# Top-32 attention followed by a quick-GELU block on one core: the division moved behind the value products, q and k turned by DMA, a second bank for the first layer, and a new order of a pair of slots

## The chip, the core and the metric

The kernel runs on one NeuronCore of one Trainium2 chip. The engines are TensorE (PE, with its weight loads as PEld), VectorE (DVE), ScalarE (ACT), GpSimd (POOL) and SyncE (SP), which issues DMAs. Each engine takes its instructions in the order in which the program gives them, and an instruction that waits holds up all that stand behind it on that engine. The metric is the device time of one execution in microseconds (us), as the median of several runs.

## The reference

Eight batches of eight heads, 576 positions, 64 values per head. Each row of scores keeps its 32 largest entries, is softmaxed over them and multiplied with v; the heads are put side by side (512 wide), and two dense layers with a gate follow.

```python
batch, n_heads, seq, head_dim = (8, 8, 576, 64)
n_tokens, d_model, d_ff = (4608, 512, 2048)
...
scores = scale * np.matmul(q, k.transpose(0, 1, 3, 2))
kth = np.partition(scores, -top_k, axis=-1)[..., -top_k:-top_k + 1]      # top_k = 32
scores = np.where(scores >= kth, scores, -1000000000.0)
attn = np.exp(scores - np.max(scores, axis=-1, keepdims=True))
attn = attn / (np.sum(attn, axis=-1, keepdims=True) + 1e-09)
x = np.matmul(attn, v)                       # heads side by side: (4608, 512)
h = x @ w_in
g = h * (1.0 / (1.0 + np.exp(-1.702 * h)))
return g @ w_out
```

## The kernel before

**Slots.** Attention is cut into 144 slots, 18 for each batch. A slot has 128 query rows of a pair of heads (`hp`, four pairs), so it has two score rows of 576 on each partition. Sixteen slots of a batch take the first 512 rows (`t` = 0 to 3 by `hp`), and two take the last 64 rows of two head pairs each ("ends" slots). Four slots with the same `t` make one tile `xT` of 128 tokens by 512 for the dense layers; the ends of two batches together make one tile `xT_t`. That gives 36 token tiles. The first layer of a tile is made in four groups (`hidden`, `ph`, 16 products in the program), and each group is projected by the second layer (`project`, `po`, four products in the program). So there are 144 groups of each, as many as slots. All products are in float32, and the trace counts each of them twice, except transposes: a group of `ph` is x32 there and a group of `po` x8.

**What a slot does.** `scores` (L240, PE) fills four banks of PSUM; `copy_scores` (L251, ACT) brings them to `sc`; `topk` (L260, L263, DVE) finds the 32 largest by four rounds of MAX8 and three of MATCH_REPLACE8 on each of the two rows; `bounds` (L279, L280, POOL) makes two numbers per row of them; `exponentials` (L288, L291, ACT) turns all scores below the 32nd to zero weight, takes the exponentials into `pr` and sums them into `den`; `divide` (L300, L302 on DVE, L310 on POOL) multiplies the whole of `pr` with the inverse of `den`; `turn_by_dma` has ACT put the low and the high halves of the words apart (L344), writes them to DRAM (L346, SP) and reads them back turned (L348, SP) into `pt`; `values` (L363, PE) multiplies with v; `bring` (L378 or L383, ACT) copies the result into `xT`. The first layer is followed by `tanh` and a copy of `ph` to `h` (L430, L433, ACT), by `gate` (L442, L443, POOL; L445 on DVE at the start and end) and by `project`; after four projections ACT copies `po` to `ob` (L465) and SP sends it out (L467).

**Order.** All orders are written out by hand. `slot(n)` handles slots 0 to 11, in which the weights are also rounded and `pr` is turned by PE (L322, L325). From slot 12 on, `two_slots(n)` handles slots n and n+1, 66 times, and two more times for what is left over; `last_slot` finishes the dense layers. In `two_slots`, the exponentials of slot n-1 come first, then `find(n)` runs on DVE with `divide(n-1)` after its seventh operation; in the second half the same follows for n and n+1. `values` takes slots n-4 and n-3. q and k of a later head pair are loaded at the slots in `FETCH` and turned by PE and ACT (`prepare`, L208 to L217) at the slots in `READY`.

**Buffers that matter.** `ps_h` has one bank, so a group of `ph` can't begin before ACT has read the last one. `ps_t` has two banks, for transposes and for `o` of `values`. `ps_p` has one for `po`. `pt` has two buffers, `sc` four, `pr` two.

Of the kernel before, what the change touches and what calls it, by code (L numbers as in the profile page):

```python
# [30 lines left out]
def kernel(  # L31
# [71 lines left out]
    apart = pool("apart", 4, space=DRAM)  # L103
    ps_s = pool("ps_s", 2, space=PSUM)
# [65 lines left out]
    def load(name, b, hp, queue=None):  # L170

        src = q if name == "q" else k
        t = loads.tile([P, NF, 2, D] if queue is None else [P, 2, NF, D], F32, name=f"{name}_l")
        heads_of = (lambda j: t[:, :, j, :]) if queue is None else (lambda j: t[:, j, :, :])
# [4 lines left out]
        if ("ends", b, hp) not in loaded:  # L179
            loaded["ends", b, hp] = loads.tile([P, 2, D], F32, name="ends")  # L180
        on = slice(0, TAIL) if name == "q" else slice(TAIL, P)
        queue.dma_start(
            loaded["ends", b, hp][on, :, :], src[b, 2 * hp : 2 * hp + 2, FULL:S, :].rearrange("h p d -> p h d")
        )
        loaded[name, b, hp] = t
# [14 lines left out]
    def prepare(name, b, hp):  # L200
        src = loaded.pop((name, b, hp))


        before = 0 if name == "q" else TAIL
        dst = qkt.tile([P, S + before], F32, name=f"{name}_t")
        full = ps_t.tile([P, 512], F32, name="tp")
        for t in range(NF):
            nc.tensor.transpose(full[:, t * P : (t + 1) * P], src[:, t, :, :], ident[:])  # L208
        scale = SCALE if name == "q" else 1.0
        nc.scalar.mul(out=dst[:, before : before + FULL], in_=full[:], mul=scale)  # L210
        (qT if name == "q" else kT)[b, hp] = dst
        if name == "k":
            ends = ps_t.tile([P, 512], F32, name="tp")
            nc.tensor.transpose(ends[:, 0:P], loaded.pop(("ends", b, hp))[:], ident[:])
            nc.scalar.mul(out=qT[b, hp][:, FULL:S], in_=ends[:, 0:TAIL], mul=SCALE)
            for to in (0, before + FULL):
                nc.scalar.copy(out=dst[:, to : to + TAIL], in_=ends[:, TAIL:P])  # L217


    slots = []  # L220
    for b in range(B):
# [3 lines left out]
        slots += ends + full if b % 2 else full + ends  # L225
# [21 lines left out]
    def copy_scores(n):  # L247
        ps = st[n].pop("ps")
        sc = st[n]["sc"] = scp.tile([P, 2, S], F32, name="sc")
        for i in range(2):  # L250
            nc.scalar.copy(out=sc[:, i, :].rearrange("p (c k) -> p c k", c=2), in_=ps[i][:, :, 0:HALF])  # L251
# [30 lines left out]
    def exponentials(n, between=lambda: None):  # L282
# [3 lines left out]
        den = st[n]["den"] = small.tile([P, 2], F32, name="den")  # L286
# [9 lines left out]
    def divide(n):  # L296

        den, pr = st[n]["den"], st[n]["pr"]
        some = small.tile([P, 2], F32, name="some")
        nc.vector.tensor_scalar_add(some[:], den[:], 1e-9)  # L300
        rden = small.tile([P, 2], F32, name="rden")
        nc.vector.reciprocal(rden[:], some[:])  # L302
        if n < SETTLED:
            by = st[n]["by"] = xtt.tile([P, 2, P], F32, name="by", tag="xT_t")
            for i in range(2):
                nc.gpsimd.tensor_scalar(by[:, i, :], ident[:], rden[:, i : i + 1], None, op0=ALU.mult)
        else:
            for i in range(2):
                on = slice(i * S, (i + 1) * S)
                nc.gpsimd.tensor_scalar(pr[:, on], pr[:, on], rden[:, i : i + 1], None, op0=ALU.mult)  # L310
# [29 lines left out]
    def turn_by_dma(n):  # L340
# [4 lines left out]
        rows = apart.tile([P, 2, 2 * S], U16, name="rows")  # L345
        nc.sync.dma_start(rows[:], halves)  # L346
        pt = st[n]["pt"] = ptp.tile([P, 2 * NF + 1, P], F32, name="pt")
# [4 lines left out]
    def values(n, put_off=None):  # L352
# [20 lines left out]
        def bring():  # L373
# [10 lines left out]
            if hps[-1] == NP - 1:  # L384
                if t < NF:
                    to = out[b * S : b * S + FULL, :].rearrange("(p t) c -> p t c", t=NF)[:, t, :]
                    ready.append((xts.pop((b, t)), [(slice(0, P), to)]))
                elif b % 2:
                    first = [(b - 1 + i) * S + FULL for i in range(2)]
                    rows = [(slice(i * TAIL, (i + 1) * TAIL), out[x : x + TAIL, :]) for i, x in enumerate(first)]  # L390
                    ready.append((xts.pop((b // 2, t)), rows))
# [6 lines left out]

    ready = []
# [4 lines left out]
    def hidden():  # L404
# [4 lines left out]
        ph = ps_h.tile([P, G, P], F32, name="ph")  # L409
# [15 lines left out]
    def tanh(aside):  # L425

        if to_gate:
            ph, g, rows = to_gate.pop()
# [21 lines left out]
    def project(blocks):  # L450
# [12 lines left out]
        if blocks[-1] == G - 1 and g == NG - 1:  # L463
            ob = thp.tile([P, C], F32, name="ob", tag="th")
            nc.scalar.mul(out=ob[:], in_=po[:], mul=0.5 / RAISE**2)  # L465
            for on, to in rows:
                nc.sync.dma_start(to, ob[on, :])  # L467
# [10 lines left out]
    READY = (((-9, -8), (-7, -6), (-4, -3), (-2, -1)), ((-8, -7), (-6, -5), (-4, -3), (-4, -3)))  # L478
    FETCH = (((-13, -12), (-11, -10), (-7, -7), (-5, -4)), ((-12, -11), (-10, -9), (-6, -6), (-5, -5)))
    VALUES = ((-8, -7, 2, 2), (-8, -7, 3, 3))  # L480
# [13 lines left out]
    for b in range(1, B):  # L494
        for hp in range(NP):
            for i, name in enumerate("qk"):
                at(b * PER + FETCH[b % 2][hp][i], load, name, b, hp)
                at(b * PER + READY[b % 2][hp][i], prepare, name, b, hp)
            at(b * PER + VALUES[b % 2][hp], load_v, b, hp)
# [16 lines left out]
    def prepare_first():  # L516

        qt = qT[0, 0] = qkt.tile([P, S], F32, name="q_t")
# [259 lines left out]
```

## Time and profile before

| | |
|---|---|
| median of 3 runs | 1820.0 us (1819.95 to 1821.7) |
| the profiled execution | 1822.16 us, of which the span of its instructions is 1820.4 us |
| PE busy | 1563.9 us (86% of the span) |
| DVE busy | 1449.2 us (80%) |
| ACT busy | 1151.6 us (63%) |
| POOL busy | 969.0 us (53%) |
| granted TensorE clock, mean | 0.93 |
| queue of SP | 42.5% of 16 DMA engines' span |

The profile page gives busy time by engine, the span in 40 slices, the DMA queues, a chain of work followed back from the last instruction, and groups of instructions by line with the idle time before them and its releaser. A timeline row has the start, the duration, the engine, the line, the operation, the count and in brackets the idle time of the engine before it with the releaser.

### The profile page before, as it was taken

The numbers are of one execution on the slowest core, as the hardware profiler recorded it, in microseconds if no ns is written. First come the engines' busy times: TensorE is split into PE (matmuls) and PEld (weight loads), VectorE is DVE, ScalarE is ACT, GpSimd is POOL, SyncE is SP. The second block draws the span as 40 slices with busy tenths as digits, with TensorE's granted clock in tenths as the row PEclk, the third lists the DMA queues.
The fourth block names the chain that finished last, engine by engine and source line by source line (L and its number), as shares of the span: only waits on it lengthen the run. The fifth ranks groups of instructions, "written<-read, shape, count | busy, mean of one in ns | idle before, by whom it ended". The sixth has DMA issues, their size and how long they took to land.

```text
span 1820.4 us, 29720 instructions
## 1 busy us (share of the span) xinstructions
PE 1563.9 (86%) x10848; PEld 1140.0 (63%) x10848; DVE 1449.2 (80%) x3220; ACT 1151.6 (63%) x2042; POOL 969.0 (53%) x909
## 2 busy tenths in 40 slices
PE   7897879888888887988888898888888888888989
PEld 5764656666666665666666666666666666666665
DVE  8998778877987787777888788777798787778840
ACT  7996655666666665566666666666666666656640
POOL 4885445555655555555555555545565555455530
PEclk8898899999999998999999998899999999899999
DMA  6443343443454443454345534345434453434430
GB/s 211 152 127 83 90 118 106 129 125 103 123 124 136 124 110 111 109 138 120 102 123 136 135 107 112 102 130 130 117 112 124 133 139 87 121 98 110 110 110 12
DMA packets 428929, 213.35 MB, mean 117 GB/s; under 512 B 394352, under 2 KB 403056, under 8 KB 428784
## 3 DMA queue, kind: packets, MB, share of 16 engines
q1 hardware_dynamic: 428352, 211.17, 42.5%
q8 instruction: 85, 1.39, 0.3%
q14 instruction: 60, 0.49, 0.1%
q10 hardware_dynamic: 432, 0.30, 0.1%
HBM read 45.09 MB, written 87.88 MB: 73 GB/s over the span
## 4 chain that ended last, share of the span: by engine, by line
PE 53%; DVE 24%; ACT 15%; POOL 6%; issue 2%; POOLq 0%; DVEq 0%; ACTq 0%
PE ph L413 22%; PE po L460 18%; DVE top L260 12%; DVE left L263 10%; PE o L363 6%; POOL pr L310 5%; PE s_ps L240 5%; ACT pr L291 5%; ACT sc L344 3%; ACT sc L288 2%; ACT ob L465 1%; ACT q_t L210 1%; PE tp L208 1%; PE tp L322 1%; ACT th L430 1%
## 5 line engine op out<-in xcount | busy, mean ns | idle before, releaser
L310 POOL TENSOR_SCALAR pr<-pr,rden 128x576 f32<-128x576 f32 x266 | 457.1, 1728 | 563.1 <-ACT th L430 408.8
L413 PE MATMUL ph<-xT,win 128*128 128x128 f32 x4096 | 565.5, 302 | 162.7 <-ACT h L433 137.8
L413 PEld LDWEIGHTS ph<-xT,win 128*128 128x128 f32 x4096 | 540.0, 215 | 236.2 <-ACT h L433 170.9
L260 DVE MAX8 top<-left 128x8 f32<-128x576 f32 x864 | 609.4, 747 | 0.0
L460 PE MATMUL po<-wout,th 128*128 128x512 f32 x1152 | 519.7, 594 | 0.7 <-ACT ob L465 0.7
L263 DVE MATCH_REPLACE8 left<-top,left 128x576 f32<-128x576 f32 x576 | 425.5, 743 | 0.0
L344 ACT COPY sc<-pr 128x2304 uint16<-128x2304 uint16 x133 | 281.1, 2114 | 220.3 <-POOL pr L310 220.2
L460 PEld LDWEIGHTS po<-wout,th 128*128 128x128 f32 x1152 | 209.6, 192 | 211.0 <-issue 209.2
L300 DVE TENSOR_SCALAR some<-den 128x2 f32<-128x2 f32 x144 | 23.4, 163 | 294.3 <-ACT pr L291 294.1
L251 ACT COPY sc<-s_ps 128x576 f32<-128x576 f32 x288 | 170.7, 649 | 94.5 <-PE s_ps L240 89.2
L291 ACT ACTIVATE pr<-sc,low 128x576 f32<-128x576 f32 x288 | 219.3, 765 | 0.0
L263 DVE MATCH_REPLACE8 left<-top,sc 128x576 f32<-128x576 f32 x288 | 211.6, 742 | 0.0
L288 ACT ACTIVATE sc<-sc,cut 128x576 f32<-128x576 f32 x288 | 207.4, 771 | 2.0 <-POOL cut L279 1.9
L260 DVE MAX8 top<-sc 128x8 f32<-128x576 f32 x288 | 202.2, 743 | 2.2 <-ACT sc L251 2.2
L240 PE MATMUL s_ps<-k_t,q_t 64*128 64x288 f32 (+1 forms) x1280 | 193.4, 451 | 7.1 <-ACT sc L251 6.9
L442 POOL TENSOR_SCALAR th<-th 128x512 f32<-128x512 f32 x129 | 192.9, 1495 | 0.0
L363 PE MATMUL o<-pt,v_l 128*64 128x128 f32 (+1 forms) x2560 | 161.0, 270 | 24.9 <-ACT xT_t L383 24.9
L443 POOL TENSOR_TENSOR th<-th,h 128x512 f32<-128x512 f32 x129 | 164.9, 1278 | 10.7
L363 PEld LDWEIGHTS o<-pt,v_l 128*64 128x64 f32 x2560 | 133.2, 141 | 57.5 <-issue 28.1
L240 PEld LDWEIGHTS s_ps<-k_t,q_t 64*128 64x128 f32 (+1 forms) x1280 | 104.6, 186 | 87.8 <-issue 25.5
L279 POOL TENSOR_SCALAR cut<-top 128x2 f32<-128x2 f32 x144 | 39.5, 275 | 205.0 <-DVE top L260 201.1
L465 ACT ACTIVATE ob<-po 128x512 f32<-128x512 f32 x36 | 21.5, 597 | 198.9 <-PE po L460 198.9
(65 smaller groups left out, 1021.8 us busy)
## 6 DMA issues: line engine op xcount, KB each, us to landing
rows<-sc SPq DMA_DIRECT2D x133, 576.0 KB, 2.8
q_l<-in_q_dram SPq DMA_DIRECT2D x64, 128.0 KB, 2.8
raw<-in_moe_w_in_dram SPq DMA_DIRECT2D x16, 512.0 KB, 4.9
v_l<-in_v_dram SPq DMA_DIRECT2D x32, 256.0 KB, 3.0
raw<-in_moe_w_out_dram SPq DMA_DIRECT2D x16, 512.0 KB, 3.6
out_dram<-ob SPq DMA_DIRECT2D x32, 256.0 KB, 2.5
k_l<-in_k_dram SPq DMA_DIRECT2D x62, 128.0 KB, 2.9
pt<-rows SPq DMA_TRANSPOSE x133, 4.6
```

The source lines that it names most:

```text
L240: nc.tensor.matmul(ps[i][rows, c, 0:HALF], lhsT=qT[b, hps[p]][on, cols], rhs=kT[b, hps[p]][on, FIRST[i] + c * HALF : FIRST[i] + (c + 1) * ...
L251: nc.scalar.copy(out=sc[:, i, :].rearrange("p (c k) -> p c k", c=2), in_=ps[i][:, :, 0:HALF])
L260: nc.vector.max(top[:, i, 8 * r : 8 * r + 8], (left if r else sc)[:, i, :])
L263: nc.vector.match_replace(left[:, i, :], top[:, i, 8 * r : 8 * r + 8], (left if r else sc)[:, i, :], LOWEST)
L288: nc.scalar.activation(sc[:, i, :], sc[:, i, :], AF.Prelu, bias=cut[:, i : i + 1], alpha=HUGE)
L291: nc.scalar.activation(pr[:, i * S : (i + 1) * S], sc[:, i, :], AF.Exp, bias=low[:, i : i + 1], accum_out=den[:, i : i + 1],)
L310: nc.gpsimd.tensor_scalar(pr[:, on], pr[:, on], rden[:, i : i + 1], None, op0=ALU.mult)
L344: nc.scalar.copy(out=halves, in_=pr[:].bitcast(U16).rearrange("p (k h) -> p h k", h=2))
L363: nc.tensor.matmul(o[j * D : (j + 1) * D, 0 : cols.stop - cols.start], lhsT=main[:, j, c, :] if c < NF else tail[:, j, :], rhs=pt[:, MAIN[ ...
L413: nc.tensor.matmul(ph[:, i, :], lhsT=win[:, c, f * P : (f + 1) * P], rhs=xT[:, c, :], start=(c == 0), stop=(c == CC - 1),)
L442: nc.gpsimd.tensor_scalar(th[:], th[:], 1.0, None, op0=ALU.add)
L460: nc.tensor.matmul(po[:], lhsT=gT[:, i, :], rhs=wout[:, f, :], start=(f == 0), stop=(f == FC - 1))
```

## The change

1. **The division is moved.** From slot 11 on `pr` isn't divided. The sums of two slots (an odd one and the next) stand in one tile `sums`; `invert` adds 1e-9 and takes the reciprocals on DVE once for a pair, and POOL spreads each over 64 columns (`wide`). PE turns `wide` into the same bank as the products with v (`sum_rows`), one copy on ACT brings both to SBUF (`x`), and POOL multiplies them into `xT` (`x_of`). `bring` is no longer used there.
2. **q and k of batches 1 to 7** are loaded into one tile and turned as `pr` is: ACT puts halves apart, four DMAs write them to DRAM and one reads them back turned (`prepare_by_dma`). The scale is applied in `copy_scores`. Batch 0 is turned by PE as before.
3. **A second bank for the first layer**: the second `hidden` of a pair takes a bank of `ps_t`.
4. **A new order of a pair**: `split` right behind the exponentials, one `tanh` behind each `hidden`, `values` of slots n-3 and n-2, `ob` put off, the ends slots ahead of the last four slots of every batch.

```diff
+    apart_qk = pool("apart_qk", 2, space=DRAM)
...
+    def prepare_by_dma(b, hp):
+        t = loaded.pop((b, hp))
+        halves = prp.tile([P, 2 * NF + 1, 2, P], U16, name="halves", tag="pr")
+        words = t[:].rearrange("p c j d -> p c (j d)").bitcast(U16)
+        nc.scalar.copy(out=halves[:], in_=words.rearrange("p c (e h) -> p c h e", h=2))
+        rows = apart_qk.tile([2 * (S + TAIL), 2, P], U16, name="qk_rows")
...
+        both = new_pair(b, hp)
+        nc.sync.dma_start_transpose(
+            out=both[:].bitcast(U16), in_=rows[0 : 2 * S + TAIL, :, :].rearrange("c h e -> (c h) e")
+        )
...
-        slots += ends + full if b % 2 else full + ends
+        slots += full[: -NP] + ends + full[-NP:]
...
-            nc.scalar.copy(out=sc[:, i, :].rearrange("p (c k) -> p c k", c=2), in_=ps[i][:, :, 0:HALF])
+            nc.scalar.mul(out=to, in_=ps[i][:, :, 0:HALF], mul=SCALE)
...
-            for i in range(2):
-                on = slice(i * S, (i + 1) * S)
-                nc.gpsimd.tensor_scalar(pr[:, on], pr[:, on], rden[:, i : i + 1], None, op0=ALU.mult)
...
+    def invert(n):
+        k = (n + 1) // 2
+        if k in sums:
+            count = 2 if 2 * k < N else 1
+            total = sums[k][:, 0:count, :]
+            nc.vector.tensor_scalar_add(total, total, 1e-9)
+            inverse = small.tile([P, 2 * count], F32, name="inverse")
+            nc.vector.reciprocal(inverse[:], total.rearrange("p s j -> p (s j)"))
+            wide = sums[k] = raws.tile([P, 2, 2, D], F32, name="wide", tag="raw")
+            nc.gpsimd.tensor_copy(
+                out=wide[:, 0:count, :, :].rearrange("p s j d -> p (s j) d"),
+                in_=inverse[:].unsqueeze(2).to_broadcast([P, 2 * count, D]),
+            )
...
+    def sum_rows(m, to):
+        nc.tensor.transpose(to, sums[(m + 1) // 2][:, (m + 1) % 2, :, :], ident[:])
...
+    def x_of(m, o, by):
...
+            nc.gpsimd.tensor_tensor(
+                out=xts[key][:, hps[p], to], in0=o[:, cols], in1=by[:, cols], op=ALU.mult
+            )
...
-        ph = ps_h.tile([P, G, P], F32, name="ph")
+        ph = (into or ps_h).tile([P, G, P], F32, name="ph", tag="tp" if into else "ph")
...
-    READY = (((-9, -8), (-7, -6), (-4, -3), (-2, -1)), ((-8, -7), (-6, -5), (-4, -3), (-4, -3)))
+    READY = (-8, -6, -4, -3)
...
         begin(first)
-        project_one()
         measure(n - 1)
-        soften(n - 1)
+        if live(n - 1):
+            exponentials(n - 1)
+            split(n - 1)
         bring_all()
+        find(n)
+        hidden()
+        project_one()
         tanh(aside)
+        prepare_some(first)
+        held = [m for m in (n - 3, n - 2) if live(m) and "rows" in st[m]]
+        o = ps_t.tile([P, 2, 2, P], F32, name="o", tag="tp") if held else None
+        for i, m in enumerate(held):
+            sum_rows(m, o[:, i, 0, :])
         if live(n + 2):
             scores(n + 2)
             copy_scores(n + 2)
-        brought = []
-        for m in (n - 4, n - 3):
-            if live(m) and "pt" in st[m]:
-                values(m, brought)
+        leave_all()
+        for i, m in enumerate(held):
+            values_at(m, o[:, i, 1, :])
+        if live(n - 1):
+            turn_by_dma(n - 1)
         if live(n + 3):
             scores(n + 3)
-        find(n)
...
         begin(second)
-        project_one()
         measure(n)
-        soften(n)
-        tanh(aside)
+        if live(n):
+            exponentials(n)
+        if held:
+            x = raws.tile([P, 2, 2, P], F32, name="x", tag="raw")
+            nc.scalar.copy(out=x[:, 0 : len(held)], in_=o[:, 0 : len(held)])
+            for i, m in enumerate(held):
+                x_of(m, x[:, i, 1, :], x[:, i, 0, :])
+        if live(n):
+            split(n)
+            turn_by_dma(n)
+        hidden(ps_t)
         if live(n + 3):
             copy_scores(n + 3)
-        prepare_some()
-        prepare_some()
-        hidden()
+        tanh(aside)
+        prepare_some(second)
+        project_one()
+        leave_all()
         find(n + 1)
-        if live(n):
-            turn_by_dma(n)
```

PE, one pair in the middle of the program before, one in which a q is turned (`tp<-ident,q_l`):

```order
L460 MATMUL po<-wout,th 128x512 x4
L240 MATMUL s_ps<-k_t,q_t 128x288 x4
L363 MATMUL o<-pt,v_l 64x128 x8
L363 MATMUL o<-pt,v_e_115 64x128 x2
L363 MATMUL o<-pt,v_l 64x128 x8
L363 MATMUL o<-pt,v_e_116 64x128 x2
L240 MATMUL s_ps<-k_t,q_t 128x288 x4
L413 MATMUL ph<-xT,win 128x128 x16
L208 MATMUL tp<-ident,q_l 128x128 x4
L460 MATMUL po<-wout,th 128x512 x4
L413 MATMUL ph<-xT,win 128x128 x16
```

PE, one pair in the middle of the changed program (`o<-ident,wide` are the turned sums):

```order
L512 MATMUL ph<-xT,win 128x128 x16
L559 MATMUL po<-wout,th 128x512 x4
L452 MATMUL o<-ident,wide 128x128 x2
L275 MATMUL s_ps<-qk_t 128x288 x4
L463 MATMUL o<-pt,v_l 64x128 x8
L463 MATMUL o<-pt,v_e_118 64x128 x2
L463 MATMUL o<-pt,v_l 64x128 x8
L463 MATMUL o<-pt,v_e_121 64x128 x2
L275 MATMUL s_ps<-qk_t 128x288 x4
L512 MATMUL ph<-xT,win 128x128 x16
L559 MATMUL po<-wout,th 128x512 x4
```

The transposes of q and k are gone and two of the sums are new; each half of a pair now has its group of `ph` ahead of a group of `po`.

ACT, two halves of pairs before, of which the first begins with the copy of `po` that leaves for the output:

```order
L465 ACTIVATE ob<-po 128x512
L288 ACTIVATE sc<-sc,cut 128x576 x2
L291 ACTIVATE pr,den<-sc,low 128x576 x2
L430 ACTIVATE th<-ph 128x512
L433 COPY h<-ph 128x512
L251 COPY sc<-s_ps 128x576 x2
L344 COPY sc<-pr 128x2304
L288 ACTIVATE sc<-sc,cut 128x576 x2
L291 ACTIVATE pr,den<-sc,low 128x576 x2
L430 ACTIVATE th<-ph 128x512
L433 COPY h<-ph 128x512
```

ACT, the second half of a pair in the changed program and the first half of the next (`x<-o` brings the products with v and the turned sums):

```order
L324 ACTIVATE sc<-sc,cut 128x576 x2
L327 ACTIVATE pr,sums<-sc,low 128x576 x2
L835 COPY x<-o 128x512
L398 COPY sc<-pr 128x2304
L287 ACTIVATE sc<-s_ps 128x576 x2
L529 ACTIVATE th<-ph 128x512
L532 COPY h<-ph 128x512
L565 ACTIVATE ob<-po 128x512
L324 ACTIVATE sc<-sc,cut 128x576 x2
L327 ACTIVATE pr,sums<-sc,low 128x576 x2
L398 COPY sc<-pr 128x2304
L529 ACTIVATE th<-ph 128x512
```

The copy that puts halves apart stands right behind the exponentials (with `x<-o` between them in the second half), and `ob` stands at the end of a half.

SP, one pair of the changed program in which q and k of two head pairs are turned:

```order
L400 DMA rows<-sc 128x2304
L243 DMA qk_rows<-halves 128x4x256 x2
L247 DMA qk_rows<-halves 128x256
L248 DMA qk_rows<-halves 64x256
L250 DMA_TRANSPOSE qk_t<-qk_rows 128x2432
L406 DMA_TRANSPOSE pt<-rows 128x9x256
L400 DMA rows<-sc 128x2304
L406 DMA_TRANSPOSE pt<-rows 128x9x256
L243 DMA qk_rows<-halves 128x4x256 x2
L247 DMA qk_rows<-halves 128x256
L248 DMA qk_rows<-halves 64x256
L250 DMA_TRANSPOSE qk_t<-qk_rows 128x2432
```

Four writes and one turning read are new for each head pair, and in the first half of a pair they stand between the write of `rows` and the turning read of `pt`.

More of the change, by code (lines that the diff above doesn't have):

```diff
@@ L200, in prepare @@
     def prepare(name, b, hp):
-        src = loaded.pop((name, b, hp))
+        src = loaded[b, hp]
+        if name == "q":
+            new_pair(b, hp)
         before = 0 if name == "q" else TAIL
-        dst = qkt.tile([P, S + before], F32, name=f"{name}_t")
+        dst = (qT if name == "q" else kT)[b, hp]
         full = ps_t.tile([P, 512], F32, name="tp")
         for t in range(NF):
-            nc.tensor.transpose(full[:, t * P : (t + 1) * P], src[:, t, :, :], ident[:])
-        scale = SCALE if name == "q" else 1.0
@@ L210, in prepare @@
-        nc.scalar.mul(out=dst[:, before : before + FULL], in_=full[:], mul=scale)
-        (qT if name == "q" else kT)[b, hp] = dst
+            nc.tensor.transpose(full[:, t * P : (t + 1) * P], of_load(name, src)[:, t, :, :], ident[:])
+        nc.scalar.copy(out=dst[:, before : before + FULL], in_=full[:])
         if name == "k":
             ends = ps_t.tile([P, 512], F32, name="tp")
-            nc.tensor.transpose(ends[:, 0:P], loaded.pop(("ends", b, hp))[:], ident[:])
-            nc.scalar.mul(out=qT[b, hp][:, FULL:S], in_=ends[:, 0:TAIL], mul=SCALE)
+            nc.tensor.transpose(ends[:, 0:P], loaded.pop((b, hp))[:, 2 * NF, :, :], ident[:])
+            nc.scalar.copy(out=qT[b, hp][:, FULL:S], in_=ends[:, 0:TAIL])
@@ L285, in exponentials @@
         pr = st[n]["pr"] = prp.tile([P, 2 * S], F32, name="pr")
-        den = st[n]["den"] = small.tile([P, 2], F32, name="den")
+        den = st[n]["den"] = sums_of(n) if n >= SETTLED else small.tile([P, 2], F32, name="den")[:]
         for i in range(2):
@@ L383, in bring @@
                     nc.scalar.copy(out=xts[b // 2, t][:, hp, at : at + TAIL], in_=o[:, 0:TAIL])
[L384 to L391, printed above, removed]
+            finish_x(n)
         if put_off is None:
@@ L463, in project, with leave, leave_all @@
         if blocks[-1] == G - 1 and g == NG - 1:
[L464 to L467, printed above, removed]
+            def leave():
+                ob = thp.tile([P, C], F32, name="ob", tag="th")
+                nc.scalar.mul(out=ob[:], in_=po[:], mul=0.5 / RAISE**2)
+                for on, to in rows:
+                    nc.sync.dma_start(to, ob[on, :])
+            leaving.append(leave)
+            if not put_off_leaving:
+                leave_all()
+    leaving = []
+    def leave_all():
+        while leaving:
+            leaving.pop(0)()
     later = {}
@@ L535, in prepare_rest @@
         for t in range(1, NF):
-            both_heads(full, loaded["q", 0, 0], t)
-        nc.scalar.mul(out=qT[0, 0][:, P:FULL], in_=full[:, P:FULL], mul=SCALE)
-        for name in ("q", "k", "ends"):
-            del loaded[name, 0, 0]
+            both_heads(full, heads_apart("q", loaded[0, 0]), t)
+        nc.scalar.copy(out=qT[0, 0][:, P:FULL], in_=full[:, P:FULL])
+        del loaded[0, 0]
     def opening():
@@ L584, in slot @@
         for fn, args in todo:
-            if fn is not prepare:
+            if fn is not prepare and fn is not prepare_by_dma:
                 fn(*args)
-        preparing = [args for fn, args in todo if fn is prepare]
+        preparing = [(fn, args) for fn, args in todo if fn is prepare or fn is prepare_by_dma]
         some = [round_piece(x) for x in by_slot.get(n, [])] if n else early
@@ L622, in slot @@
         if n < NP:
-            for args in preparing:
-                prepare(*args)
+            for fn, args in preparing:
+                fn(*args)
         if n >= TURNS:
@@ L688, in find @@
                 op()
-                if i == 6 and live(m - 1):
-                    divide(m - 1)
+                if i == 2 and m % 2 == 0:
+                    invert(m - 2)
                 if i > 1 and unfinished:
```

163 lines of the change are left out of this document (106 added, 57 removed).

## The prediction

> **What bounds the kernel now.** I read the engines' busy time, then the groups with the idle time before them, then the chain of waits.
>
> ```profile
> PE 1563.9 (86%) x10848; PEld 1140.0 (63%) x10848; DVE 1449.2 (80%) x3220; ACT 1151.6 (63%) x2042; POOL 969.0 (53%) x909
> ...
> PE 53%; DVE 24%; ACT 15%; POOL 6%; issue 2%; POOLq 0%; DVEq 0%; ACTq 0%
> ...
> L413 PE MATMUL ph<-xT,win 128*128 128x128 f32 x4096 | 565.5, 302 | 162.7 <-ACT h L433 137.8
> ...
> L300 DVE TENSOR_SCALAR some<-den 128x2 f32<-128x2 f32 x144 | 23.4, 163 | 294.3 <-ACT pr L291 294.1
> ...
> L465 ACT ACTIVATE ob<-po 128x512 f32<-128x512 f32 x36 | 21.5, 597 | 198.9 <-PE po L460 198.9
> ```
>
> No engine is full. DVE works 1449 us and loses 294 us at one place: the first instruction of `divide` (L300) waits for the exponentials on ACT. PE loses 138 us waiting for ACT to empty the one bank of `ph`. ACT waits 199 us ahead of `ob` for a projection. The chain of waits shows how these hang together over four slots (start, duration, what):
>
> ```profile
> 901.37 0.60 ACT ob L465
> 901.96 0.71 ACT sc L288 x2
> ...
> 903.19 1.62 ACT pr L291 x4
> ...
> 904.84 0.18 DVE some L300
> ...
> 905.04 0.15 DVE rden L302
> ...
> 924.48 3.44 PE po L460 x8
> 927.92 3.57 PE ph L413 x32
> 931.49 3.44 PE po L460 x8
> 934.92 1.17 PE s_ps L240 x8
> 936.10 2.33 PE o L363 x40
> 938.43 1.17 PE s_ps L240 x8
> 939.60 3.77 PE ph L413 x32
> 943.37 3.45 PE po L460 x8
> ...
> 946.84 0.60 ACT ob L465
> ```
>
> PE makes five groups and the products between them without a gap from 924.48 to 946.82; `ob` waits for the last; the exponentials stand behind `ob`, DVE behind the exponentials. The ring from `ob` to `ob` takes 946.84 − 901.37 = 45.5 us, though neither engine works that long in it. The timeline gives what a search costs when nothing waits, and what a gap costs PE:
>
> ```profile
> 145.70 1.41 DVE L260 MAX8 top<-sc 128x8 f32<-128x576 f32 x2
> ...
> 904.84 0.17 DVE L300 TENSOR_SCALAR some<-den 128x2 f32<-128x2 f32 x1 [3.74 <-ACT pr L291]
> ...
> 905.81 5.47 PE L413 MATMUL ph<-xT,win 128*128 128x128 f32 x32 [4.48 <-ACT h L433]
> ...
> 914.75 0.16 DVE L300 TENSOR_SCALAR some<-den 128x2 f32<-128x2 f32 x1
> ...
> 921.09 3.39 PE L413 MATMUL ph<-xT,win 128*128 128x128 f32 x28 [1.06 <-ACT xT L378]
> ...
> 924.66 0.16 DVE L300 TENSOR_SCALAR some<-den 128x2 f32<-128x2 f32 x1
> ...
> 1740.02 4.76 PE L413 MATMUL ph<-xT,win 128*128 128x128 f32 x28 [2.89 <-ACT xT L378]
> ...
> 1748.69 0.67 DVE L445 SCALAR_TENSOR_TENSOR th<-th,h 128x512 f32<-128x512 f32 x1
> ```
>
> From 914.75 to 924.66 DVE does one search with its division: 9.91 us. The division is 904.84 to 905.19, 0.35 us, so a search is **9.56 us**. Slot 12's search begins at 145.70 and the last ends at 1748.69: 66 pairs in 1603 us, **24.3 us a pair**, of which DVE needs 2 × 9.91 = 19.8. What stands ahead of 145.70 isn't changed in its order, apart from the scale moving from one ACT copy to another.
>
> **The change, part by part.** These rows carry prices:
>
> ```profile
> L310 POOL TENSOR_SCALAR pr<-pr,rden 128x576 f32<-128x576 f32 x266 | 457.1, 1728 | 563.1 <-ACT th L430 408.8 <-DVE rden L302 146.3 <-ACT sc L251 8.0
> ...
> L344 ACT COPY sc<-pr 128x2304 uint16<-128x2304 uint16 x133 | 281.1, 2114 | 220.3 <-POOL pr L310 220.2
> ...
> L251 ACT COPY sc<-s_ps 128x576 f32<-128x576 f32 x288 | 170.7, 649 | 94.5 <-PE s_ps L240 89.2 <-DMA rows<-sc 5.0
> ...
> L442 POOL TENSOR_SCALAR th<-th 128x512 f32<-128x512 f32 x129 | 192.9, 1495 | 0.0
> L443 POOL TENSOR_TENSOR th<-th,h 128x512 f32<-128x512 f32 x129 | 164.9, 1278 | 10.7
> ...
> L430 ACT ACTIVATE th<-ph 128x512 f32<-128x512 f32 x144 | 84.1, 584 | 46.7 <-PE ph L413 46.5
> ...
> L208 PE MATMUL tp<-ident,q_l 128*128 128x128 f32 x124 | 19.5, 281 | 2.4 <-ACT k_t L210 1.7 <-DMA q_l<-in_q_dram 0.6
> ...
> L280 POOL TENSOR_TENSOR low<-top 128x2 f32<-128x2 f32 x144 | 28.8, 200 | 0.0
> ...
> L214 PE MATMUL tp<-ident,ends 128*128 128x128 f32 x31 | 10.1, 327 | 19.4 <-ACT q_t L210 18.1 <-ACT k_t L210 1.3
> ```
>
> *DVE.* The wait at L300 goes: `invert` needs only sums made half a pair earlier, behind which 9.56 us of search have run (were they late, the search queued behind it would wait). Two divisions become one `invert` with the same two operations: a pair is 2 × 9.56 + 0.35 = 19.47 us, **66 pairs 1285 us**. What is late next is the copy of scores. `find(n+2)` needs a copy that stands a pair ahead, so PE may fall about 10 us (one search) behind before DVE waits.
>
> *PE.* In the new order 8 groups of `ph` stand ahead of slot 12 and 9 behind the last search, so 127 between; of `po` 4, 10 and 130. By the chain a group of `ph` is 3.57 to 3.77 us, of `po` 3.44, scores 1.17, values of two slots 2.33. That is 127 × 3.67 + 130 × 3.44 + 146 × 1.17 + 146 × 1.17 (132 slots, 14 ends slots counted twice) + 131 transposes of sums × 0.16 (L208: 19.5/124) = 466 + 447 + 171 + 171 + 21 = **1276 us**. Turning a sum could cost what L214 shows, 0.33, so +22 us; or nothing, if it hides in a gap. The PE work that goes (28 × 9 transposes, 28 × (8 × 0.157 + 0.327) = 44 us) is simply not in this sum. So PE and DVE need nearly the same, 1276 and 1285.
>
> *Where PE still waits.* Of the 34 tiles made by pairs, 17 are needed the moment they are complete: `hidden` in the second half stands right behind the last `x_of`. Its path from the end of the first scores of that pair: copy of scores 2 × 0.6, exponentials 2.85 (901.96 to 904.81), copy `x` about 0.58 (as L430, the same shape), `x_of` on POOL, handovers of some 0.3. For `x_of` there is no row of 128x128 with two inputs; L280 with two columns takes 0.20 and L443 with 512 takes 1.28. I take 0.5, nearer to L280 by its size. Together 5.4 us, against 2.33 + 1.17 us of values and scores that PE does meanwhile: **1.9 us × 17 = 32 us**, 27 to 46 by those ends. The other 17 tiles have a pair to spare, because an ends slot completes no tile in an even batch and one too many in an odd one.
>
> *The clock.* After a gap of 4.48 us the group at 905.81 takes 5.47 instead of 3.6, and after 2.89 us 28 products take 4.76 instead of the 3.39 at 921.09, where the gap was 1.06. So a gap of 1.9 costs between 0 and 1.4 to 1.9 us; I take half, **15 us** for 17. The Trainium skill ("TensorE: Matmul & The Clock Gate", Part 1: The HAM clock gate) says that the array falls to half rate after an idle window of about 3.4 us. By that rule these 17 gaps would cost nothing and the sum would be 15 us less. The gap of 4.48 us agrees with it, the one of 2.89 us doesn't.
>
> *POOL.* 457 us of L310 go; new are 66 copies to 256 columns and 149 `x_of`. Per half it has about 0.4 + 1.50 + 1.28 us of other work (two small ones as L280, then L442 and L443), so the copies (0.2 to 1.5) are hidden by 3.44 us of projection; without that cover they would cost up to 66 × 1.5 = 99 us. `x_of` waits for ACT's `x`, and behind it stand the next bounds, a search later.
>
> *ACT.* Out: `prepare` and `bring`; in: 28 copies of 2304 halves at 2.11 (L344) and 67 `x`. Per pair 2 × (2.85 + 2.11 + 1.2 + 1.15) + 0.6 + 0.3 for `ob` + 0.9 for q and k = 16.4 us, under 19.5. It waits in three new places: for `ph` at `tanh`, for `o` at `x`, and for the projection at `ob`, behind which the next exponentials stand. In the last case PE still has `ph`, `po`, sums, scores and values ahead of it, 3.7 + 3.4 + 0.3 + 1.2 + 2.3 = 10.9 us, while ACT does 0.6 + 2.85 + 2.11 + 1.15 + 1.2 = 7.9, or 10.0 with a copy of q and k. It is hidden, by 1 us in the worst case.
>
> *SP and the DMA.*
>
> ```profile
> SPq L348 <- DMA rows<-sc: 353.5, 133, 4.6
> ```
>
> ```profile
> rows<-sc SPq DMA_DIRECT2D x133, 576.0 KB, 2.8
> ...
> pt<-rows SPq DMA_TRANSPOSE x133, 4.6
> ```
>
> ```profile
> L348 SPq DMA_TRANSPOSE pt<-rows x133: 2252/2515/3969, 161.1 to 1762.4; - x133
> ```
>
> A turned pair of q and k adds four writes and a turning read of about the size of `pt` (2432 against 2304 columns). On SP that is some 2 us of issue, 2.8 of waiting for the write and 2.5 of the turning read, 7.3 us, 28 times; behind it stand `ob`'s output and the reads of `pt`. `pt` of slot n lands some 3 + 4.6 us behind its split and is used a good half pair after, about 5 us to spare, and what is held up in a first half is the `pt` of slot n−1, which has 10 us more. I take **nothing**, and as the other end 28 × 3 = 84 us.
>
> *The tail.* Behind the last search PE has 9 × 3.67 + 10 × 3.44 = 67 us, values and sums 4, and the last five projections stand right behind their own `ph`, each waiting for `tanh` 0.58 and the gate on DVE 0.67 with handovers, 1.5 × 5 = 7; then `ob` and the output, 3: **81 us** (before: 1820.4 − 1748.7 = 72).
>
> **The sum.** 145.7 + 1276 + 32 + 15 + 81 = 1550 us of span; DVE alone would give 145.7 + 1285 + 81 = 1512, so PE is the later one. The profiled execution took 1.8 us more than its span and 2.2 more than the median of the runs; the two cancel. Forecast **1550 us**.
>
> **The rivals.**
> - *PE loses nothing and DVE alone sets the pace:* 1512 us. For it: PE may be 10 us late before DVE waits. Against it: PE has too little slack (9 us in 66 pairs) to make up 17 waits. With the 17 gaps waited for but free of any half clock the sum is 1550 − 15 = 1535, between the two. That is the time by the rule of the Trainium skill above (same page and part).
> - *ACT becomes the ring,* because it now waits for PE in three places of a pair: its worst half has 1 us of cover. If each pair loses 2 us to this, 145.7 + 66 × 22 + 81 = 1679. For it: 294 us of DVE's waiting came from just such a place. Against it: 16.4 us of work in 19.5.
> - *The second bank brings nothing,* so the change doesn't do what it says: the 138 us at L413 stay, 1550 + 138 − 32 = 1656. Against it: the bank is read half a pair before it is needed again.
> - *SP holds `pt` back:* in 28 places q and k are queued ahead of it. It decides from about 10 us a place beyond the 7.3 + 5 above: 28 × 10 = 280 gives 1830, slower than before. Against it: 353.5 us over 133 waits for `rows` is 2.7 us each, and the longest is 4.6.
>
> **How the numbers follow.** Forecast (1520 to 1600) 0.55; DVE alone 0.12; ACT's ring 0.22; bank 0.05; SP 0.05; nothing to be seen 0.01. The range goes down to 1505, DVE alone with transposes hidden. Upward the unknown costs add 22 (sums), 14 (`x_of`), 15 (clock), 84 (SP) in part; with half of the ACT cases inside, 1660 leaves out about 2 in 10. A measurement of this kernel can tell about 0.2% from no change. Faster 0.94, same 0.01, slower 0.05.
>
> **What would show it.** DVE's idle time ahead of the operation that replaces L300 near zero; searches 19.5 to 20.3 us a pair; PE's waits for `h` gone and 17 waits of about 2 us for POOL's `xT` in their place; granted clock above 0.93; about 81 us behind the last search. The forecast is wrong if DVE waits for copies of scores all through (PE or ACT is the ring), if PE waits for `pt` landing, or if the half-clock stretches stay as many as they were.

## The result, and the profile after

The changed kernel takes **1575.2 us** (median of four runs, 1571.6 to 1582.1), against 1820.9 of the kernel before beside it: a ratio of **0.8654, 95% interval 0.8624 to 0.8685**. The forecast was 1550, its range 1505 to 1660. The profiled execution is the longest of the four: 1582.1 us, its span 1580.2.

From the page of the changed kernel: the engines, the clock, the main DMA queue, and the group of `x_of` with its idle time:

```profile
PE 1469.7 (93%) x10729; PEld 1064.5 (67%) x10729; DVE 1434.8 (91%) x3090; ACT 1172.8 (74%) x1846; POOL 590.0 (37%) x855
...
PEclk8899899999999999999999999999999999999999
...
q1 hardware_dynamic: 533184, 246.05, 59.5%
...
L481 POOL TENSOR_TENSOR xT<-x 128x128 f32<-128x128 f32 x117 | 51.7, 457 | 348.2 <-ACT x L835 288.8
```

DVE works nearly as long as before (1449 us there), in 240 us less, and the clock stands at 0.97 over the span, above the 0.93 that I had asked for. The waits of DVE, PE and POOL come from the list of waits (engine, line, what was waited for: total us, times, longest):

```profile
POOL xT L481 <- PE ph L512: 55.3, 6, 9.3
...
DVE top L296 <- ACT sc L287: 37.5, 13, 5.0
...
PE o L463 <- DMA pt<-rows: 30.1, 13, 4.8
...
PE po L559 <- POOL th L542: 24.6, 8, 3.8
...
DVE sums L357 <- ACT pr L327: 15.6, 14, 1.2
...
PE ph L512 <- POOL xT L481: 13.9, 13, 4.3
```

The 294 us of DVE ahead of `divide` have shrunk to 15.6 ahead of `sums`, and PE's wait for `h` is gone from the list. New are DVE's 37.5 us for copies of scores. Rows of DVE's timeline cut the span into three: the first operation of slot 12's search, the beginnings of three searches in a row between which nothing waits (with the `invert` of that pair), and the last operation of the last search.

```profile
145.16 1.41 DVE L296 MAX8 top<-sc 128x8 f32<-128x576 f32 x2
...
953.50 1.40 DVE L296 MAX8 top<-sc 128x8 f32<-128x576 f32 x2
...
963.14 1.40 DVE L296 MAX8 top<-sc 128x8 f32<-128x576 f32 x2
...
965.18 0.16 DVE L357 TENSOR_SCALAR sums<-sums 128x4 f32<-128x4 f32 x1
...
973.05 1.40 DVE L296 MAX8 top<-sc 128x8 f32<-128x576 f32 x2
...
1489.44 1.41 DVE L296 MAX8 top<-left 128x8 f32<-128x576 f32 x2
```

The last search ends at 1489.44 + 1.41 = 1490.85. So 66 pairs take 1345.7 us, 20.39 each. Where nothing waits a search takes 963.14 − 953.50 = 9.64 us and one with `invert` 973.05 − 963.14 = 9.91, a pair 19.55 and 66 of them 1290.3. The span is then 145.2 + 1290.3 + **55.4 of waiting** + **89.3 behind the last search** = 1580.2.

The 55 us aren't spread evenly. In the stretches in which the tiles are needed the moment they are complete, which I had priced at 32 us of waits and 15 of clock, a pair takes what DVE needs: from 948 to 1027 DVE is busy for 78.86 of 79 us and PE for 77.51. DVE waits half a microsecond or more for a copy of scores in twelve places, in and at the edges of the stretches of which the forecast said that a tile has "a pair to spare". One of them, on POOL and then on PE and DVE:

```profile
469.74 0.45 POOL L481 TENSOR_TENSOR xT<-x 128x128 f32<-128x128 f32 x1 [9.30 <-PE ph L512]
470.16 0.22 POOL L315 TENSOR_SCALAR cut<-top 128x2 f32<-128x2 f32 x1
470.35 0.19 POOL L316 TENSOR_TENSOR low<-top 128x2 f32<-128x2 f32 x1
470.51 1.49 POOL L541 TENSOR_SCALAR th<-th 128x512 f32<-128x512 f32 x1
472.08 1.27 POOL L542 TENSOR_TENSOR th<-th,h 128x512 f32<-128x512 f32 x1
```

```profile
465.92 3.73 PE L512 MATMUL ph<-xT,win 128*128 128x128 f32 x32
473.41 6.40 PE L559 MATMUL po<-wout,th 128*128 128x512 f32 x8 [3.75 <-POOL th L542]
```

```profile
481.98 1.42 DVE L296 MAX8 top<-sc 128x8 f32<-128x576 f32 x2 [3.64 <-ACT sc L287]
```

`x_of` starts a new tile in a pool of two buffers. PE still reads the older one, until its group at 465.92 ends. POOL works in order, so the bounds of the next slot and the gate of the next projection stand behind the 9.3 us. PE finds `th` unready, loses 3.75 us, and does the projection in 6.40 us instead of 3.60. The scores that follow come late, DVE's cover is used up, and it waits 3.64. There are six such waits of POOL, and DVE waits behind each of them, 25 us in all. About as much lies elsewhere, mostly behind PE's 13 waits for `pt` landing.

### The profile page after: what moved, and what is told of

Read it like the earlier page. It is cut to its first block, busy times and chain, and to the rows that moved or that the text cites. A ratio compares the mean times of both kernels' runs of the same rounds, so it can differ in the third digit from the quotient of the medians.

```text
span 1580.2 us, 29328 instructions
## 1 busy us (share of the span) xinstructions
PE 1469.7 (93%) x10729; PEld 1064.5 (67%) x10729; DVE 1434.8 (91%) x3090; ACT 1172.8 (74%) x1846; POOL 590.0 (37%) x855
## 3 DMA queue, kind: packets, MB, share of 16 engines
q1 hardware_dynamic: 533184, 246.05, 59.5%
## 5 line engine op out<-in xcount | busy, mean ns | idle before, releaser
L559 PE MATMUL po<-wout,th 128*128 128x512 f32 x1152 | 532.4, 606 | 31.7 <-POOL th L542 24.6
L512 PEld LDWEIGHTS ph<-xT,win 128*128 128x128 f32 x4096 | 477.7, 193 | 72.3 <-issue 55.2
L512 PE MATMUL ph<-xT,win 128*128 128x128 f32 x4096 | 492.5, 278 | 13.9 <-POOL xT L481 13.9
L287 ACT ACTIVATE sc<-s_ps 128x576 f32<-128x576 f32 x288 | 171.7, 651 | 149.2 <-PE s_ps L275 132.0
L296 DVE MAX8 top<-sc 128x8 f32<-128x576 f32 x288 | 202.4, 745 | 37.5 <-ACT sc L287 37.5
L275 PE MATMUL s_ps<-qk_t 64*128 64x288 f32 (+1 forms) x1280 | 189.9, 444 | 2.0 <-ACT sc L287 1.6
L481 POOL TENSOR_TENSOR xT<-x 128x128 f32<-128x128 f32 x117 | 51.7, 457 | 348.2 <-ACT x L835 288.8
L463 PE MATMUL o<-pt,v_l 128*64 128x128 f32 (+1 forms) x2384 | 150.1, 271 | 30.1 <-DMA pt<-rows 30.1
L463 PEld LDWEIGHTS o<-pt,v_l 128*64 128x64 f32 x2384 | 124.0, 142 | 59.7 <-DMA pt<-rows 33.5
L529 ACT ACTIVATE th<-ph 128x512 f32<-128x512 f32 x144 | 86.2, 599 | 93.9 <-PE ph L512 93.9
L275 PEld LDWEIGHTS s_ps<-qk_t 64*128 64x128 f32 (+1 forms) x1280 | 103.0, 183 | 44.5 <-issue 22.6
L532 ACT COPY h<-ph 128x512 f32<-128x512 f32 x128 | 75.3, 588 | 0.0
```

Of the source, the lines that this page charges most:

```text
L275: nc.tensor.matmul(ps[i][rows, c, 0:HALF], lhsT=qT[b, hps[p]][on, cols], rhs=kT[b, hps[p]][on, FIRST[i] + c * HALF : FIRST[i] + (c + 1) * ...
L287: nc.scalar.mul(out=to, in_=ps[i][:, :, 0:HALF], mul=SCALE)
L296: nc.vector.max(top[:, i, 8 * r : 8 * r + 8], (left if r else sc)[:, i, :])
L463: nc.tensor.matmul(o[j * D : (j + 1) * D, cols], lhsT=main[:, j, c, :] if c < NF else tail[:, j, :], rhs=pt[:, MAIN[j] + c if c < NF else ...
L512: nc.tensor.matmul(ph[:, i, :], lhsT=win[:, c, f * P : (f + 1) * P], rhs=xT[:, c, :], start=(c == 0), stop=(c == CC - 1),)
L559: nc.tensor.matmul(po[:], lhsT=gT[:, i, :], rhs=wout[:, f, :], start=(f == 0), stop=(f == FC - 1))
```

## The experiments

Times are medians, with the ratio to the kernel before in the same job. The first four change the kernel after.

**A third buffer for the tile** (`raws` gives up one of eight to make room):

```diff
-    raws = pool("raws", 8)
+    raws = pool("raws", 7)
...
-    xtp = pool("xtp", 2)
+    xtp = pool("xtp", 3)
```

> The changed kernel with three buffers for POOL's xT instead of two (and seven for raws instead of eight, to make room). Theory A (POOL's x_of waits for PE to read an old tile out of a pool of two; the next bounds and the gate queue behind it): the six waits of POOL for ph, 55 us together, are gone, with them PE's six waits of 3.75 us ahead of po and DVE's waits of 2 to 4 us for sc that follow; 1575 falls to between 1540 and 1555. Theory B (what costs the 55 us of DVE's waiting is pt landing late, because SP turns q and k ahead of it; POOL's waits lie in time that PE would lose anyway): DVE's waiting stays at about 55 us and the time between 1568 and 1580. Theory C (DVE is the pace and a pair is 20.4 us whatever the waits are): unchanged within 3 us.

Measured: 1556.3 us, 0.8547 [0.8533, 0.8561]; 19 us less. The list of waits of this kernel:

```profile
PE o L463 <- DMA pt<-rows: 36.4, 14, 5.0
...
DVE top L296 <- ACT sc L287: 18.2, 6, 5.7
```

POOL's wait for `ph` and PE's for POOL's `th` are gone from the list, and DVE's wait is halved. So theory A is right in kind and just misses its band: 19 us, where it had 20 to 35. What is left begins with `pt`.

**No turning of q and k** in later batches:

```diff
-        t = loaded.pop((b, hp))
-        halves = prp.tile([P, 2 * NF + 1, 2, P], U16, name="halves", tag="pr")
...
+        loaded.pop((b, hp))
+        qT[b, hp], kT[b, hp] = qT[0, hp], kT[0, hp]
```

> The changed kernel without the turning of q and k of batches 1 to 7: the first batch's q and k stand in for them (their loads stay), so ACT's 28 copies and the DMAs to DRAM and back are left out. Theory B (SP turns q and k ahead of pt): PE's 30 us of waits for pt landing fall below 5, DVE's waits behind them go, and the time falls by 20 to 40 us, to 1535 to 1555. Theory A (POOL's xT): the six waits of POOL for ph stay at about 9 us each and the time falls by under 20 us. My forecast had priced this turning at nothing, with 84 us as the other end.

Measured: 1543.5 us, 0.8477 [0.8463, 0.8492]; 32 us less. In its list of waits no wait for `pt` is left, and POOL's are still there:

```profile
POOL xT L466 <- PE ph L497: 54.9, 6, 9.3
...
DVE top L281 <- ACT sc L272: 11.7, 4, 4.2
```

So both causes are real. Their effects, 19 and 32 us by medians, are of the size of what was lost: the 55 us are those of the profiled execution, which is 7 us above the median. But they aren't two separate shares. Without the turning only three of POOL's six waits still reach DVE, where all six did with it.

**One bank for both hidden layers:**

```diff
-        hidden(ps_t)
+        hidden()
```

> The changed kernel with both hidden layers of a pair in the one bank of ph, as before the change. If the second bank is what took away PE's 138 us of waits for h, they come back, 2 us a pair or more, and the time rises by 100 to 138 us, to 1675 to 1715. If the new order (tanh right behind its own hidden, half a pair ahead of the next) took them away by itself, PE's waits for h stay under 10 us and the time stays between 1570 and 1590.

Measured: 1575.3 us, 0.8652 [0.8638, 0.8667]: no difference from the changed kernel. PE's wait for the bank, in the list of this kernel:

```profile
PE ph L512 <- ACT h L532: 3.5, 4, 1.2
```

It was 138 us on the page of the kernel before (155.7 in its list of waits). The other parts took it away without the bank; the order (`tanh` right behind its own `hidden`) is the likely one, but it wasn't tried alone.

**q and k of later batches turned by PE again:**

```diff
     def prepare_by_dma(b, hp):
 
-        t = loaded.pop((b, hp))
...
+        for name in "qk":
+            prepare(name, b, hp)
```

> The changed kernel with q and k of the later batches turned by PE, through a bank of PSUM and ACT, as before the change (at the places in the program where the change has its copies). PE gets its 44 us of transposes back (28 times 1.58 us). Theory B (SP and the DMA): PE's waits for pt fall below 5 us, so that the time comes out within 15 us of the changed kernel, or below it. If the turning by DMA is worth what it takes from PE, the time rises by 30 to 50 us, to 1605 to 1625.

Measured: 1592.8 us, 0.8744 [0.8731, 0.8757]; 17.6 us more, between the two theories. PE's wait for `pt` falls from 30.1 to 2.3 us, but its 44 us of transposes are back. Turning by DMA takes 44 us of work from PE (the forecast's estimate) and puts 28 us of waits in its place.

The next four start from the kernel before, to see which part made DVE's wait go.

**The second bank alone:**

```diff
-        hidden()
+        hidden(ps_t)
         find(n + 1)
```

> The kernel before with the second hidden layer of each pair in a bank of its own (part 3 alone). If the ring is ob, exponentials, divide, search (the theory of the forecast), PE's 138 us of waits for h vanish from their place but come back ahead of another product of PE, and the time stays within 25 us of 1820. If the one bank is itself a link of the ring, the time falls by 70 to 138 us, to 1680 to 1750.

Measured: 1820.9 us, 1.0002 [0.9992, 1.0012]. The list of waits of the kernel before, and two rows of this kernel's, show why:

```profile
PE ph L413 <- ACT h L433: 155.7, 44, 4.5
```

```profile
DVE some L300 <- ACT pr L291: 296.7, 58, 12.0
...
PE o L363 <- ACT h L433: 141.3, 44, 5.2
```

PE's wait for `h` has moved from `ph` to the values' `o`, which take the next bank of that pool, and is nearly as long as it was: 141.3 us against 155.7. DVE's wait is unchanged.

**`ob` put off alone:**

```diff
             copy_scores(n + 2)
+        leave_all()
...
             copy_scores(n + 3)
+        leave_all()
```

> The kernel before with the output copy ob put off on ACT behind the copies of scores, in both halves (a piece of part 4 alone). If the ring is ob, exponentials, divide, the exponentials no longer wait for the projection, DVE's 294 us ahead of divide fall below 150, and the time falls by 80 us or more, below 1740. If DVE's wait has another source (the bounds or the scores come late by themselves), the time stays within 30 us of 1820.

Measured: **1648.6 us**, 0.9053 [0.9039, 0.9066]; 172 us of the 246 that the whole change brings, from the place of one ACT copy of 0.6 us that is made 36 times. DVE's and PE's waits:

```profile
DVE some L300 <- ACT pr L291: 125.0, 48, 7.4
...
PE ph L413 <- ACT h L433: 20.8, 21, 1.3
```

With the exponentials no longer behind the projection, PE's wait for `h` falls too: it was a link of the same ring.

**`ob` put off, and `divide` at the end of the search:**

```diff
-                if i == 6 and live(m - 1):
+                if i == 13 and live(m - 1):
```

> The kernel before with ob put off as in the run beside it, and with divide at the end of the search instead of half way into it, so that the sums have half a search more to come. If the wait at divide is what holds DVE, both together come near the changed kernel without moving the division: 1600 to 1680. If the normalised exponentials on GpSimd (1.73 us an instruction, four a pair, behind divide) then hold up the turned rows, PE waits for pt, and the time is above 1700.

Measured: 1653.1 us, 0.9076 [0.9063, 0.9090]. It lies in the band of the first theory, but only because `ob` does: moving `divide` on top of that gains nothing, and DVE still waits 124.0 us for the exponentials. Half a search more isn't what they lack; what they wait for in this order wasn't taken further.

**The division alone** (part 1 of the change in the old order; values, sums and `x_of` as in the change):

```diff
-                if i == 6 and live(m - 1):
-                    divide(m - 1)
+                if i == 2 and m % 2 == 1:
+                    invert(m - 3)
...
-                values(m, brought)
+                values_divided(m, brought)
```

> The kernel before with part 1 alone: the division behind the values, on GpSimd, the order otherwise as it was. If taking divide off DVE's path is what the change lives on, DVE's 294 us ahead of it go to under 60 and the time comes to 1600 to 1700 (PE's waits for h remain and are next). If ACT's ring through ob holds by itself (exponentials behind ob behind the projection), the wait moves to DVE's first instruction of a search, for the copy of scores, and the time stays above 1740.

Measured: 1782.7 us, 0.9788 [0.9774, 0.9803]; 38 us less. The second theory has the time right, and the place in part:

```profile
ACT ob L547 <- PE po L542: 228.3, 36, 13.2
...
DVE sums L324 <- ACT pr L291: 158.3, 54, 4.5
...
DVE top L260 <- ACT sc L251: 100.1, 46, 3.5
```

The 294 us have become 158 ahead of `sums`, where DVE still waits for the exponentials, and 100 ahead of the search itself, where the theory had them all. The ring through `ob` holds without the division in it.

**The changed kernel with `ob` at once:**

```diff
-                project(range(G), True)
+                project(range(G), False)
```

> The changed kernel with ob not put off: ACT empties po right behind the projection, ahead of tanh in the first half and of the next pair's work in the second, where it stood already. If ob ahead of ACT's other work is what made the ring before, the time rises by 40 us or more, above 1615. If in the new order the place of ob no longer matters (exponentials of the pair stand ahead of it, and the division is off DVE's path), it stays within 15 us of 1575.

Measured: 1574.2 us, 0.8654 [0.8635, 0.8672]: no difference. So the change breaks the ring without `ob` put off, and `ob` put off breaks most of it without the change. The division alone and the second bank alone don't, so in the change it is most likely the order, in which the exponentials of each half stand ahead of its projection; that order wasn't tried by itself.

**q and k behind `pt` on SP**, with the third buffer; the fourth turning comes a slot later, so that no pair has two:

```diff
+        def turn_both():
...
+            put_off.append(turn_both)
...
-    READY = (-8, -6, -4, -3)
+    READY = (-8, -6, -4, -2)
...
             turn_by_dma(n - 1)
+        while turning:
+            turning.pop(0)()
```

> The changed kernel with three buffers for xT, and with the DMAs of q and k moved on SP behind the turning read of that half's slot (the fourth pair of heads a pair later, so that no pair has two). If POOL's xT and SP's order are the two causes of the 55 us that DVE waits, and add up, a pair comes to 19.55 us from slot 12 to the last search and the time to 145 + 66 times 19.55 + 89 + 2 = 1526 (1522 to 1532). If the turning by DMA disturbs pt by the traffic itself, whatever its place on SP, PE's waits for pt stay at 20 us or more and the time above 1540.

Measured: 1569.8 us, 0.8622 [0.8607, 0.8637]: **13 us more** than with the third buffer alone. The first theory's 1526 is missed. The figures of the second, waits of 20 us or more and a time above 1540, are met: PE's waits for `pt` rose to 49.5 us. But its reason, the traffic, isn't what the rows show. The timeline of the SP queue (start, duration of the issue, what):

```profile
680.70 2.33 SPq L411 DMA_TRANSPOSE pt<-rows  x1
683.08 1.12 SPq L244 DMA_DIRECT2D qk_rows<-halves  x2
...
688.84 2.96 SPq L251 DMA_TRANSPOSE qk_t<-qk_rows  x1
691.84 0.59 SPq L197 DMA_DIRECT2D v_l<-in_v_dram  x1
...
696.94 0.63 SPq L186 DMA_DIRECT2D qk_l<-in_k_dram  x1
697.67 0.54 SPq L405 DMA_DIRECT2D rows<-sc  x1
700.90 2.76 SPq L411 DMA_TRANSPOSE pt<-rows  x1
```

and ACT and PE in the same place:

```profile
683.86 2.12 ACT L403 COPY sc<-pr 128x2304 uint16<-128x2304 uint16 x1
```

```profile
706.44 1.97 PE L468 MATMUL o<-pt,v_l 128*64 128x128 f32 x16 [5.64 <-DMA pt<-rows]
```

ACT has split the next slot at 685.98, but its `rows` leave at 697.67: SP is held by the turning until 691.80, which waits for its own write to land, and then spends 5.8 us on issuing nine loads of q, k and v. Moved out of the way of one slot's `pt`, the turning stood in the way of the next slot's `rows`.

**The last slots' order**, on top of that:

```diff
         gate(False)
+        hidden(ps_t if hidden_at["g"] % 2 else None)
         if may_project(0):
             project(range(G))
-        hidden()
```

> As the run beside it, and with the last slots' order changed: the next hidden layer ahead of each projection, in alternating banks, so that PE works while tanh and the gate run. The five waits of 1.4 us of PE for DVE's th go: 7 us less than the run beside it, about 1519 (1515 to 1526). If PE is held by something else there (the bank, the clock), the two are alike.

Measured: 1563.4 us, 0.8586 [0.8573, 0.8598]; 6.4 less than the run beside it, where 7 was expected; the 1519 itself was missed with its base. PE's five waits for DVE's `th` are gone from the list.

**q and k written ahead of `pt`, turned behind it, and the loads spread:**

```diff
+        nc.sync.dma_start(rows[2 * S : 2 * S + TAIL, :, :], halves[TAIL:P, 2 * NF, :, :])
+
         def turn_both():
...
             both = new_pair(b, hp)
             nc.sync.dma_start_transpose(
...
-    READY = (-8, -6, -4, -2)
-    FETCH = (-12, -10, -7, -5)
-    VALUES = (-8, -7, 1, 2)
+    READY = ((-8, -6, -4, -2), (-14, -12, -4, -2))
+    FETCH = ((-12, -10, -6, -4), (-18, -16, -10, -8))
+    VALUES = (-5, -6, 1, 3)
```

> As the kernel with the new tail, but q and k are written to DRAM at their first place on SP, ahead of pt, and only their turning read stands behind pt; the turnings and the loads of q, k and v are spread, so that from the second batch on no pair has both a turning and the loads of q and k. In the run that moved everything behind pt the next slot's rows stood on SP behind 8.7 us of turning and 5.8 us of issuing loads, 11.7 us late in one look. If this queue is what is left, PE's waits for pt fall below 12 us and the time to 1519 to 1530. If the DMA traffic itself makes pt late, PE's waits for pt stay above 20 us and the time above 1545.

Measured: **1512.6 us** (five runs, 1512.2 to 1513.0), 0.8306 [0.8295, 0.8317]: 62.5 us less than the changed kernel, and 6 below the band. Its page and its waits:

```profile
PE 1449.4 (96%) x10729; PEld 1055.9 (70%) x10729; DVE 1430.3 (95%) x3090; ACT 1175.3 (78%) x1846; POOL 589.1 (39%) x855
...
q1 hardware_dynamic: 533184, 246.05, 61.9%
```

```profile
PE ph L518 <- POOL xT L487: 19.5, 17, 3.7
...
PE o L469 <- DMA pt<-rows: 2.7, 2, 1.5
```

```profile
146.63 1.41 DVE L302 MAX8 top<-sc 128x8 f32<-128x576 f32 x2
...
1435.40 1.41 DVE L302 MAX8 top<-left 128x8 f32<-128x576 f32 x2
```

66 pairs take 1436.81 − 146.63 = 1290.2 us, 19.55 each: DVE waits for nothing. The span of 1510.9 leaves 74.1 behind the last search, 8 less than the 82 that the changed kernel's 89 and the new order's 7 make, since PE is less far behind when DVE ends. The queue carried the same 246.05 MB as in the changed kernel, and the read of `pt` landed a median 4.7 us behind its issue in both. So neither the amount of traffic nor slower reads made `pt` late; it was the time at which SP came to issue it. Which of the two edits here, the split of write and read or the spreading, does more wasn't separated.

## Why the prediction was right, and where it was off

The mechanism held: DVE's wait for ACT's exponentials went, DVE and PE became nearly equal, and the time came within 1.6% of the forecast. By its steps:

- *The ring from `ob` to `ob`* was read rightly. Putting off `ob` alone is worth 172 us, the division alone 38, the second bank alone nothing. Between the 1648.6 of `ob` alone and the 1575.2 of the change lie 73 us. The turning of q and k by DMA is 17.6 of them; the rest belongs to division and order together and wasn't taken apart.
- *DVE: 19.47 us a pair.* 19.55 where nothing waits, 5 us in all: a search without the division takes 9.64 us, not 9.56. *POOL's prices* held too: `x_of` 0.457 us where I took 0.5.
- *PE: 1276 us of work in 66 pairs.* PE was busy for 1257.8 us of them in the last experiment, 18 less. So DVE, not PE, is the later one.
- *17 gaps of 1.9 us, and 15 us for the clock* were one step that failed. PE's waits for `xT` are 13.9 us in 13 places, most of them 0.7 to 0.8 us; in the last experiment 19.5 in 17, the forecast's count, and there DVE loses nothing to them. I had added PE's waits to PE's work, though the slack for them was larger than the 9 us that I saw: it was 32 between 1290 and 1258. In that run the term costs nothing, not 47.
- *"The other 17 tiles have a pair to spare"* is the sentence that failed most. It looked at when a tile is needed and not at when its buffer comes free. I had noted that bounds queue behind `x_of`, but only asked how long `x_of` waits for ACT. The third buffer, one edit, is worth 19 us.
- *SP and the DMA: nothing, other end 84.* It cost 32 us, the difference that leaving the turning out makes (ACT's 28 copies go with it, but the last experiment keeps them and loses nothing). I counted 7.3 us a turning, and 5 to 10 us of spare time, and forgot the loads of q, k and v that stand beside the turnings in the same queue, 5.8 us of issuing in the rows above.
- *The tail: 81 us.* 89 in the changed kernel. The five waits of 1.4 us were sized rightly (the new order of the last slots takes 6.4 away); the other 8 are work that PE was behind when DVE ended: behind the last search PE was busy for 78.2 us in the changed kernel and 69.7 in the last experiment.
- *The rivals.* "DVE alone" at 1512 is what the kernel comes to without the two queues' waits: 1512.6. That they agree so closely is luck: the pairs take 5 us more than the rival had, and the tail, with its new order, 7 less. "The second bank brings nothing" was true of the bank and false of its price: the rest of the change does what the bank was to do. "ACT becomes the ring" isn't seen: DVE waits for ACT in some places and not in each pair, and `ob` at once changes nothing. "SP holds `pt` back" was the right mechanism at a tenth of its price.
- *The signs.* DVE's old wait is near zero, PE's wait for `h` is gone, and the clock is above 0.93, as forecast. A pair took 20.39 us, just outside the 19.5 to 20.3. And one of the three signs of being wrong did show: PE waits 30.1 us for `pt` landing, of which the list of the kernel before has nothing.

The terms were off in both directions: 47 us for PE's waits and clock that cost nothing, and 55 us of waits in two places that were taken as free. So that the forecast is within 1.6% is in part luck: it is nearer to the result than its working was.

## What to carry to other kernels

An engine's queue is a resource of its own: for each instruction that a change adds, ask what stands behind it, and whether it waits for a buffer as well as for its data. When two engines need nearly the same time, waits of the one are free as long as they fit into the slack that the other leaves in that place; adding them all to the work counts them twice. Bunched, they cost sooner: six waits of 3.75 us each reached DVE here, and 17 mostly shorter ones, spread out, did not in the last experiment. Moving a blocking transfer behind one user of its queue puts it ahead of the next one: split it into the part that waits and the part that doesn't, and spread the rest.

## What the runs showed of the hardware

Equal gaps of PE did not have equal consequences. Rows of PE's timeline in the changed kernel, each for a projection of eight products, the first without a gap and the others behind one:

```profile
462.49 3.60 PE L559 MATMUL po<-wout,th 128*128 128x512 f32 x8
...
580.55 5.40 PE L559 MATMUL po<-wout,th 128*128 128x512 f32 x8 [1.87 <-POOL th L542]
...
845.68 6.29 PE L559 MATMUL po<-wout,th 128*128 128x512 f32 x8 [3.75 <-POOL th L542]
...
890.42 3.70 PE L559 MATMUL po<-wout,th 128*128 128x512 f32 x8 [3.75 <-POOL th L542]
```

Of the six gaps of 3.74 or 3.75 us in this kernel four were followed by 6.29 to 6.70 us and two by 3.70; one of 1.87 was followed by 5.40. The granted clock over these projections goes with them: 0.68 at 580.55, 0.58 at 845.68, 1.00 at 890.42. In values, a gap of 3.27 us was followed by 1.98 us for 16 products that take 1.09 at full clock. Behind a gap of 2.34 they took 1.09, but the scores a microsecond later took 2.29 instead of 1.24, at a granted clock of 0.50:

```profile
335.96 1.98 PE L463 MATMUL o<-pt,v_l 128*64 128x128 f32 x16 [3.27 <-DMA pt<-rows]
...
1081.93 1.09 PE L463 MATMUL o<-pt,v_l 128*64 128x128 f32 x16 [2.34 <-DMA pt<-rows]
...
1083.24 2.29 PE L275 MATMUL s_ps<-qk_t 64*128 64x288 f32 x8
```

So the length of the gap alone doesn't decide whether PE slows down, nor when. The Trainium skill ("TensorE: Matmul & The Clock Gate", Part 1: The HAM clock gate) puts the drop behind an idle window of about 3.4 us, and says that the window is free-running. The rows at 335.96, 580.55 and 1081.93 lie below that length and the clock drops all the same, which that rule doesn't foretell; the one at 890.42 lies above it and the clock stays, which a free-running window may leave room for.

The five runs of the last experiment agree within 0.8 us, the four of the changed kernel only within 10.5. What spreads them wasn't looked for; waiting alone doesn't, since the four runs with `ob` put off alone, in which DVE waits 125 us, agree within 1.6.
